# A fused attention and gated-MLP block: head sums in larger batches, a longer token ring, and another order of the first loads

## The chip, the cores and the metric

The kernel runs on one core of a Trainium2 chip. A core has five engines that run side by side, each through its own list of instructions in order: TensorE (PE, matrix products into PSUM), VectorE (DVE), ScalarE (ACT), GpSimd (POOL) and SyncE (SP), which here only issues DMA transfers. They meet through semaphores. SBUF is the working memory; PSUM has eight banks of 128 partitions by 512 fp32 values. The metric is the device time of one execution in microseconds, the median of some runs.

## The reference

x has 2048 tokens of 640 features. Everything is computed on the layer-normalised tokens, and two branches are added to x:

```python
x = A_x
xn = _layernorm(x, axis=-1)
return x + _A_ref(xn, A_wqkv, A_wo) + _B_ref(xn, B_w_gate, B_w_up, B_w_down)
```

Branch A is attention with 32 heads of 20 features, in which a token sees only eight keys: itself and the tokens 2, 4, ... 14 before it.

```python
off = jnp.arange(W) * dil                       # W = 8, dil = 2
idx = pos[:, None] - off[None, :]
logits = jnp.einsum("bhsd,bhswd->bhsw", q, kg) * scale      # kg: k gathered at idx
logits = jnp.where(mask[None, None, :, :], logits, -1e9)    # mask: idx >= 0
attn = _softmax(logits, axis=-1)
o = jnp.einsum("bhsw,bhswd->bhsd", attn, vg)                # vg: v gathered at idx
```

Branch B is (xn @ w_gate) * (xn @ w_up) @ w_down with 1536 inner features.

## The kernel before

**A planner orders everything.** The kernel's parts are generators that yield tasks (an engine, what is read and written, a priority, how many PSUM banks are needed). `Sched.run` simulates the engines with estimated durations, and at each step gives an engine the ready task of the best priority (a small number is better). What comes out is a fixed list of instructions for each engine, and the semaphore waits between them are derived from the tiles read and written (`deps_of`). The estimates set only the order; on the chip an engine waits for what is really missing, and everything behind it on that engine waits too.

**Tiling.** Tokens come in 16 tiles of 128 and 4 blocks (j) of 512. Features come in 5 chunks (c) of 128, so that a chunk of q, k or v holds 4 of each head's 20 features for all 32 heads.

**Stages, in the order in which the data needs them:**

1. *Front* (`front`, one for each tile t): the x tile is loaded into a ring `XST` of `NXS` = 8 slots. VectorE takes statistics (L511, L514), ScalarE a square root (L517), VectorE normalises into `XNS` (L521, L522). Tiles 0 to 4 are transposed by TensorE (L541) and copied out by VectorE (L549); tiles 5 to 15 are transposed by DMA (L556). The result is `XNT`, features on partitions. A tile from 8 on is loaded only when the tile eight before it has been normalised.
2. *Projections* (`mms`, L579): q and k of blocks 0 and 1 in small pieces as tiles come, then q and k of blocks 2 and 3, and v (`proj_v`) for each block; ScalarE empties the banks (L584). v goes to DRAM (`store_v`), since it is read back shifted.
3. *Head products and sums*: for each block and each half r of the eight key offsets, VectorE multiplies q with four shifted k (L702), one instruction for each chunk, into one of 8 product slots `PRD`. `logits` sums them over each head's features: 20 narrow matmuls (32 output columns, four abreast in the array) for one block and half, L718, into one bank, which ScalarE empties into `LOG` (L728). There are 8 such batches. A product slot is free again when its matmuls are done.
4. *Softmax* for two blocks at a time on VectorE, with the exponential on ScalarE; the weights move by DMA into `ATX`.
5. *Weighted values*: for each unit u = (block, chunk), 20 in all, four shifted pieces of v are loaded into a ring `VX`, VectorE multiplies them with the weights, which stand in two PSUM banks (L861), GpSimd adds pairs into `SV` (L866), and TensorE sums with 8 narrow matmuls a unit (`sums`, L905); ScalarE empties the bank into `OT` (L914). Two units make one batch.
6. *Gate and up* (`gu`, L945): for each block 12 groups of two times 5 matmuls; ScalarE empties the gate's bank, VectorE multiplies it with the up bank (L954).
7. *Output* (`dn`, L1000): for each block 8 groups of 17 matmuls (12 from branch B, 5 from `OT`); VectorE adds x (L1011) and SyncE stores. A block's outputs start when all 5 of its units are summed.

**Order of the start.** SyncE issues x tile 0, then the five chunks of the q weights one by one with x tile 2 between, then the k weights in two pieces with x tile 3 between; ScalarE's own queue issues x tile 1. TensorE meanwhile runs dummy matmuls on zeros (`warm`, L563): nine of 512 columns at the start and three behind the first tile's transposes.

Much memory is shared over time: `VST` (v before its store) and the ring `XST` lie in `OT`, the product slots in the down weights and others.

Of the kernel before, what the change touches and what calls it, by code (L numbers as in the profile page):

```python
# [3 lines left out]
FP32 = mybir.dt.float32  # L4
# [5 lines left out]
D = 640  # L10
# [9 lines left out]
NJ = 4  # L20
# [15 lines left out]
class _Op:  # L36
    __slots__ = ("eng", "fn", "deps", "needs_tick", "event", "pre_know", "dma", "name", "idx", "end", "group")

# [10 lines left out]
class Sched:  # L49
# [5 lines left out]
    def __init__(self, nc):  # L55
        self.nc = nc
        self.ops = []
        self.state = {}
        self.base = {}
        self.clock = {e: nc.alloc_semaphore(f"clk_{e}") for e in ("act", "pe", "dve", "pool")}  # L60
        self.n_dma = 0
        self.t = {"sp": 0.8, "act": 0.8, "pe": 1.26, "dve": 0.9, "pool": 0.8}
        self.t_lock = 0.0
        self.t_data = 0.0
        self.pe_mode = 0
        self.threads = []
        self.banks = {b: 0.0 for b in range(8)}
        self.seq = 0
        self.groups = {}

    def sbuf(self, name, shape, dtype, offset):
# [33 lines left out]
    def deps_of(self, eng, rk, wk):  # L105
        deps = {}
        inorder = eng in ("pe", "act", "dve")
        for k in rk:
            st = self.state.get(k)
            if st is not None and st[0] is not None:  # L110
                deps[st[0].idx] = st[0]
        for k in wk:
            st = self.state.get(k)
            if st is None:
                continue
            o, rds = st
            if o is not None and not (eng == "pe" and o.eng == "pe"):
                deps[o.idx] = o
            for q in rds:
                if inorder and q.eng == eng and not q.dma:  # L120
                    continue
                deps[q.idx] = q
        return deps

    def op(self, eng, fn, r=(), w=(), dma=False, name="", occ=None, lat=None, lock=False, nbytes=0, mode=0, group=None):
        X = _Op()
        X.eng, X.fn, X.name, X.dma, X.group = eng, fn, name, dma, group
        X.needs_tick, X.event, X.pre_know, X.idx = False, None, None, len(self.ops)
        rk = [k for a in r for k in self.keys(a)]
        wk = [k for a in w for k in self.keys(a)]  # L130
# [10 lines left out]
        if dma:  # L141
            self.t[eng] = start + (0.48 if occ is None else occ)
            self.t_data = max(self.t_data, start + 1.2) + nbytes / 280e3
            X.end = self.t_data + 0.8
        else:
            self.t[eng] = start + occ
            X.end = start + (occ if lat is None else lat)
# [190 lines left out]
def build_kernel(nc, A_x, A_wqkv, A_wo, B_x, B_w_gate, B_w_up, B_w_down, out):  # L338
# [5 lines left out]
    def sb(name, shape, dtype=BF16, at=None):  # L344
# [4 lines left out]
        if at is None:  # L349
# [13 lines left out]
    VST = sb("VST", [128, NJ, NCH, JB], at=a_ot)  # L363
    NXS = 8
    XST = sb("XST", [128, NXS, D], at=a_ot + 2 * NCH * JB * 2)
    a_qk = place[0]
    QT = sb("QT", [128, NJ, NCH, JB])
    KT = sb("KT", [128, NCH, VL])
    NVX = 5
    VX = sb("VX", [128, NVX, 4, VW], at=a_qk)  # L370
# [5 lines left out]
    PRD += [sb(f"PRD{5 + i}", [128, 4, JB]) for i in range(3)]  # L376
    NS = 3
    SV = [sb(f"SV{i}", [128, 4, JB], at=a_pr + i * 4096) for i in range(NS)]
    a_sc = place[0]
# [5 lines left out]
    RS = sb("RS", [128, 2, TS], at=a_sc + 4096)  # L385
    PV = [sb("PV0", [128, 2, 2, JB], FP32, at=a_qk + 20864), sb("PV1", [128, 2, 2, JB], FP32, at=a_qk + 20864 + 8192),
          sb("PV2", [128, 2, 2, JB], FP32, at=a_sc)]
    NP = len(PV)
    LOG = [sb(f"LOG{i}", [128, 2, W, TS]) for i in range(2)]
    HX = [sb(f"HX{i}", [128, JB], at=place[0] - 8192 + i * 1024) for i in range(8)]  # L390
    HX += [sb(f"HX{8 + i}", [128, JB]) for i in range(4)]
    ATX0 = sb("ATX0", [128, 2, 2, JB])
    ATX = [ATX0, sb("ATX1", [128, 2, 2, JB])]
    NXR = 3
    a_xr = place[0]
# [31 lines left out]
    def num(n, *k):  # L427
        return lambda: count.get(k, 0) >= n
# [23 lines left out]
    op("pool", lambda e: e.memset(KT[:, :, 0:PAD], 0.0), w=[KT[:, :, 0:PAD]], name="kpad", occ=0.3)  # L452

    def x_load(t, eng="sp"):
        dma(XST[:, t % NXS, :], xhbm[t * TS:(t + 1) * TS, :], w=[XST[:, t % NXS, :]], name=f"xld{t}", eng=eng)
        mark("x", t)
# [7 lines left out]
    def loads():  # L464
        def t(f, *a):
            return Task("sp", lambda: f(*a), prio=0)

        for t_ in range(4, NXS):
            yield t(x_load, t_)
        for t_ in range(NXS, NT):  # L470
            yield have("apply", t_ - NXS)
            yield t(x_load, t_)
            if t_ == NXS + 2:
                yield t(wqkv_load, 2)

# [12 lines left out]
    def late_loads():  # L488
        yield num(2 * NJ, "lg")

# [11 lines left out]
    def front(t):  # L502
        x, st = XST[:, t % NXS, :], STATS[:, t, 0:12]
        xs, mv = XNS[:, t % NXN, :], MV[:, t, 0:2]
# [49 lines left out]
        else:  # L554
            def dmat():
                op("sp", lambda e: e.dma_start_transpose(o, xs), r=[xs], w=[o], dma=True, name=f"dtr{t}", nbytes=200e3, occ=1.25)  # L556

# [3 lines left out]
    def warm(n):  # L561
        for _ in range(n):
            op("pe", lambda e: e.matmul(PS[:, 7, :], ZERO[:, 0:128], ZERO[:], start=True, stop=True),  # L563
               r=[ZERO[:]], w=[PS[:, 7, :]], name="warm", occ=0.4 if n > 3 else 0.25)

# [83 lines left out]
    def proj_v(j, m):  # L649
# [11 lines left out]
        for t in range(4 * j, 4 * j + 4):  # L661
            yield have("xnt", t)
        if j >= 2:
            for t in range(NT):
                yield have("apply", t)
        yield Task("pe", go, r=[WQKV[:, 2, 4, 0:64], XNT[:, NCH - 1, j * JB:(j + 1) * JB]], prio=30 + j, banks=1)
# [15 lines left out]
    def products():  # L682
        n = 0
        for j, r in pairs:
            slots = []
            for c in range(NCH):
                for which in (0, 1):
                    yield num(4, "qk", which, j, c)
                    if which == 1 and j > 0:
                        yield num(4, "qk", 1, j - 1, c)  # L690
                if n >= 8:
                    yield have("prd", n - 8)
                s = PRD[n % 8]
                base = KT[:, c, :]
# [10 lines left out]
                yield Task("dve", go, r=[q, rk], w=[s[:]], prio=20 + j, lock=True)  # L705
                slots.append((n, s))
                n += 1
            K.spawn(logits(j, r, slots))

    def logits(j, r, slots):  # L710
        hold = []

        def go(b):
            for c, (n, s) in enumerate(slots):
                for a in range(4):
# [5 lines left out]
                mark("prd", n)  # L721
            hold.append(b)

        dst = LOG[j // 2][:, j % 2, 4 * r:4 * r + 4, :]

        def ev():
            b = hold[0]
            X = op("act", lambda e: e.activation(dst, PS[:, b, :].rearrange("p (q s) -> p q s", q=4), ACT.Copy, scale=SCALE), r=[PS[:, b, :]], w=[dst],  # L728
                   name=f"lgev{j}_{r}", occ=0.58)
            K.free_bank(b, X)  # L730
# [6 lines left out]

        yield Task("pe", go, r=[slots[-1][1][:]], prio=9.5, banks=1, slack=0.5)
        bump("lg")
        yield Task("act", ev, r=[PS[:, hold[0], :]], w=[dst], prio=2)  # L740
        bump("logits", j // 2)

    def softmax(x):
# [35 lines left out]

        yield num(4, "logits", x)  # L780
        if x:
# [16 lines left out]
    def vx_loads():  # L798
        yield num(2 * NJ, "lg")
        for u in range(NU):  # L800
# [15 lines left out]

    at_bank = []
    used = [-3, -2, -1]

# [10 lines left out]
    def unit(u):  # L830
# [60 lines left out]
        mark("mul", u)  # L891
        if u % 2 == 1:
            K.spawn(sums((u - 1, u)))

    def sums(us):
# [22 lines left out]

        yield Task("pe", go, r=[SV[u % NS][:] for u in us], prio=9.7, banks=2, slack=0.7)
        yield Task("act", ev, r=[PS[:, b, :] for b in hold], prio=3)  # L920

    def gu(j):
# [5 lines left out]
        elif j == 1:  # L928
            for jj in range(NJ):
                yield num(NCH, "v", jj)  # L930
        elif j == 2:
            yield have("atx", 1)
        else:
            yield num(8, "dn", j - 3)
# [179 lines left out]
```

## Time and profile before

| | us |
|---|---|
| median of 3 runs (274.76 to 275.71) | 275.2 |
| the profiled execution, its own time | 276.79 |
| its span in the trace | 275.1 |

| engine | busy us | largest groups of instructions (line, busy us) |
|---|---|---|
| TensorE | 266.8 | gate and up L945 117.1; output L1000 84.5; projections L579 67.8; head sums L718 10.1; value sums L905 6.2; dummies L563 5.5 |
| VectorE | 222.9 | weighted values L861 92.8; products L702 46.1; gate times up L954 24.3 and more |
| GpSimd | 95.4 | pair sums L866 93.8 |
| ScalarE | 93.6 | emptying PSUM L584, L728, L914 |

Busy time of TensorE counts pipelined matmuls from start to modelled end, so a run of 20 is given some 0.1 to 0.2 us longer than the distance to the next start; distances between starts are the safer measure. How full the span is, in 40 slices of 6.9 us (a digit is the busy share in tenths):

```profile
PE   6997999999999999999999999999999999999995
...
DVE  4676789999999979999999999999799999423221
ACT  2355667555754245224243302221033201142000
POOL 1000000000000000197847976699656877500000
...
DMA  6959348802122899968423447535561012200101
```

Some transfers of the start, from issue to landing: x tile 0 (160 KB) 3.1 us from 0.81; x tile 1, on ScalarE's queue, 2.9 us from 0.81; the five q weight chunks (160 KB each) 2.9 to 5.1 us; k weights 5.9 (480 KB) and 6.2 us (320 KB); v weights (800 KB), issued at 12.42, 5.9 us.

### The profile page before, as it was taken

The numbers are of one execution on the slowest core, as the hardware profiler recorded it, in microseconds if no ns is written. First come the engines' busy times: TensorE is split into PE (matmuls) and PEld (weight loads), VectorE is DVE, ScalarE is ACT, GpSimd is POOL, SyncE is SP. The second block draws the span as 40 slices with busy tenths as digits, with TensorE's granted clock in tenths as the row PEclk, the third lists the DMA queues.
The fourth block names the chain that finished last, engine by engine and source line by source line (L and its number), as shares of the span: only waits on it lengthen the run. The fifth ranks groups of instructions, "written<-read, shape, count | busy, mean of one in ns | idle before, by whom it ended". The sixth has DMA issues, their size and how long they took to land.

```text
span 275.1 us, 4416 instructions
## 1 busy us (share of the span) xinstructions
PE 266.8 (97%) x1761; PEld 151.1 (55%) x1781; DVE 222.9 (81%) x285; ACT 93.6 (34%) x169; POOL 95.4 (35%) x57
## 2 busy tenths in 40 slices
PE   6997999999999999999999999999999999999995
PEld 2796965444444444444444576466744576444773
DVE  4676789999999979999999999999799999423221
ACT  2355667555754245224243302221033201142000
POOL 1000000000000000197847976699656877500000
PEclk9999999999999999999999999999999999999999
DMA  6959348802122899968423447535561012200101
GB/s 191 308 170 147 80 86 268 334 2 80 44 84 52 232 212 238 290 121 207 107 52 84 121 112 189 153 80 165 148 167 24 1 50 75 68 2 0 48 26 48
DMA packets 39492, 33.47 MB, mean 122 GB/s; under 512 B 15024, under 2 KB 38192, under 8 KB 39472
## 3 DMA queue, kind: packets, MB, share of 16 engines
q1 hardware_dynamic: 39328, 33.03, 45.6%
q8 instruction: 14, 0.23, 0.4%
q10 hardware_dynamic: 144, 0.16, 0.2%
q14 instruction: 6, 0.05, 0.1%
HBM read 25.07 MB, written 5.26 MB: 110 GB/s over the span
## 4 chain that ended last, share of the span: by engine, by line
PE 94%; DMA 3%; DVE 1%; issue 1%; ACT 0%; SPq 0%
PE PS L945 38%; PE PS L1000 27%; PE PS L579 22%; PE PS L718 3%; PE PS L905 2%; DMA XNT<-XNS 2%; DMA XST<-in_A_x_dram 1%; PE PS L541 1%; PE PS L563 0%; DVE XNT L549 0%; DVE XNS L522 0%; DVE STATS L511 0%; ACT SD L517 0%; DVE FOUT L1011 0%; DVE SD L521 0%
## 5 line engine op out<-in xcount | busy, mean ns | idle before, releaser
L866 POOL TENSOR_TENSOR SV<-PV 128x1024 bf16<-128x1024 f32 x40 | 93.8, 2358 | 87.8 <-DVE PV L861 87.6
L861 DVE TENSOR_TENSOR PV<-VX,PS 128x1024 f32<-128x1024 bf16 (+1 forms) x56 | 92.8, 1671 | 1.4 <-ACT PS L846 1.4
L579 PE MATMUL PS<-XNT,WQKV 128*128 128x512 bf16 (+2 forms) x473 | 67.5, 302 | 2.7 <-DMA XNT<-XNS 1.6
L945 PE MATMUL PS<-XNT,WG 128*128 128x512 bf16 x237 | 59.2, 379 | 0.2
L579 PEld LDWEIGHTS PS<-XNT,WQKV 128*128 128x128 bf16 x480 | 44.3, 115 | 25.6 <-DMA XNT<-XNS 2.1
L945 PE MATMUL PS<-XNT,WU 128*128 128x512 bf16 x230 | 57.9, 379 | 0.4
L702 DVE TENSOR_TENSOR PRD<-QT,KT 128x2048 bf16<-128x2048 bf16 x40 | 46.1, 1218 | 0.0
L1000 PE MATMUL PS<-WD,HT 128*128 128x320 bf16 x288 | 43.1, 299 | 0.0
L584 ACT ACTIVATE HT<-PS 128x512 bf16<-128x512 f32 x36 | 21.4, 596 | 54.8 <-PE PS L945 54.8
L945 PEld LDWEIGHTS PS<-XNT,WU 128*128 128x128 bf16 x240 | 23.1, 98 | 29.1 <-issue 1.7
L945 PEld LDWEIGHTS PS<-XNT,WG 128*128 128x128 bf16 x240 | 23.2, 98 | 28.7 <-issue 1.3
L954 DVE TENSOR_TENSOR HT<-HT,PS 128x512 bf16<-128x512 bf16 x36 | 24.3, 684 | 14.6 <-PE PS L945 14.4
L1000 PEld LDWEIGHTS PS<-WD,HT 128*128 128x128 bf16 x288 | 27.9, 98 | 12.3 <-issue 1.3
L1011 DVE TENSOR_TENSOR FOUT<-PS,XR 128x320 bf16<-128x320 f32 x32 | 15.6, 488 | 19.2 <-PE PS L1000 19.2
L1000 PE MATMUL PS<-WO,OT 128*128 128x320 bf16 x160 | 27.0, 299 | 0.0
L914 ACT ACTIVATE OT<-PS 128x512 bf16<-128x512 f32 x20 | 10.8, 596 | 35.6 <-PE PS L905 35.6
L736 POOL MEMSET LOG<- 32x6 bf16 (+6 forms) x7 | 0.4, 95 | 53.7 <-ACT LOG L728 53.7
L1000 PEld LDWEIGHTS PS<-WO,OT 128*128 128x128 bf16 x160 | 15.7, 98 | 6.1
L584 ACT ACTIVATE QT<-PS 128x512 bf16<-128x512 f32 (+1 forms) x22 | 12.3, 557 | 12.4 <-PE PS L579 12.4
L511 DVE BATCH_NORM_STATS2 STATS<-XST 128x6 f32<-128x320 bf16 x32 | 13.9, 477 | 2.7 <-DMA XST<-in_A_x_dram 2.7
L584 ACT ACTIVATE HX<-PS 128x512 bf16<-128x512 f32 x12 | 7.2, 597 | 25.7 <-PE PS L945 25.7
L584 ACT ACTIVATE KT<-PS 128x512 bf16<-128x512 f32 (+1 forms) x22 | 12.3, 557 | 7.9 <-PE PS L579 7.9
(43 smaller groups left out, 130.7 us busy)
## 6 DMA issues: line engine op xcount, KB each, us to landing
VX<-v_scratch SPq DMA_DIRECT2D x80, 130.0 KB, 2.9
v_scratch<-VST SPq DMA_DIRECT2D x4, 640.0 KB, 4.5
XR<-in_A_x_dram SPq DMA_DIRECT2D x16, 160.0 KB, 2.8
XST<-in_A_x_dram SPq DMA_DIRECT2D x15, 160.0 KB, 4.4
out_dram<-FOUT SPq DMA_DIRECT2D x15, 160.0 KB, 1.8
WG<-in_B_w_gate_dram SPq DMA_DIRECT2D x1, 1920.0 KB, 7.8
WU<-in_B_w_up_dram SPq DMA_DIRECT2D x1, 1920.0 KB, 11.8
WD<-in_B_w_down_dram SPq DMA_DIRECT2D x1, 1920.0 KB, 13.5
```

The lines of the kernel that those rows point to most:

```text
L511: op("dve", (lambda o, a: lambda e: e.bn_stats(o, a))(o, a), r=[a], w=[("st", t, i)], name=f"bn{t}_{i}", occ=0.49)
L579: op("pe", (lambda o, l, x, c, first: lambda e: e.matmul(o, l, x, start=first, stop=(c == NCH - 1)))(o, l, x, c, first), r=[l, x], w=[o], ...
L584: X = op("act", (lambda o, i: lambda e: e.activation(o, i, ACT.Copy))(o, i), r=[i], w=[o], name=name, occ=0.12 + n * 0.9e-3)
L702: op("dve", lambda e: e.tensor_tensor(s[:], qb, kv, ALU.mult), r=[q, rk], w=[s[:]], name=f"prod{j}_{r}_{c}", occ=1.15, lock=True)
L718: op("pe", (lambda o, x, a, c: lambda e: e.matmul(o, G[:], x, start=(c == 0), stop=(c == NCH - 1), tile_position=(0, 32 * a)))(o, x, a, c) ...
L861: op("dve", lambda e: e.tensor_tensor(p, vw, a, ALU.mult), r=[vv] + rk, w=[p], name=f"pv{u}_{x}_{r0}", occ=0.09 + 1.1 * nr)
L866: X = op("pool", lambda e: e.tensor_tensor(o, p[:, :, 0, :], p[:, :, 1, :], ALU.add), r=[p[:]], w=[o], name=f"pva{u}_{x}", occ=2.36, lock= ...
L914: X = op("act", (lambda o, b: lambda e: e.activation(o, PS[:, b, :], ACT.Copy))(o, b), r=[PS[:, b, :]], w=[o], name=f"oev{u}", occ=0.58)
L945: op("pe", (lambda l, x, c: lambda e: e.matmul(PS[:, b, :], l, x, start=(c == 0), stop=(c == NCH - 1)))(l, x, c), r=[l, x], w=[PS[:, b, :] ...
L954: X = op("dve", lambda e: e.tensor_tensor(h, h, PS[:, hold[1], :], ALU.mult), r=[h, PS[:, hold[1], :]], w=[h], name=f"h{m}_{j}", occ=0.65)
L1000: op("pe", (lambda l, x, i: lambda e: e.matmul(PS[:, b, 0:DHALF], l, x, start=(i == 0), stop=(i == n - 1)))(l, x, i), r=[l, x], w=[PS[:, b ...
L1011: X = op("dve", lambda e: e.tensor_tensor(o, PS[:, b, 0:DHALF], xr, ALU.add), r=[PS[:, b, :], xr], w=[o], name=f"fin{t}_{nb}", occ=0.49)
```

## The change

Seven edits go together:

- **Head sums once a block**: `logits` takes both halves of a block, ten slots, into two banks: 4 batches of 40 narrow matmuls. There are twelve product slots, the four new ones in memory that is free at that time; every twelfth product waits for the last token tile to be transposed, and gate/up of block 1 for all head sums (a slot lies in its `HT`).
- **Value sums for three units**: six batches of three units (three banks) and a last one of two. `SV` has five slots instead of three, `VX` four instead of five.
- **Token ring of twelve**: x tiles 4 to 11 are issued without waiting, then the v weights, then tiles 12 to 15. The ring now lies also where v of block 1 is put, so v of block 1 waits for tiles 8 to 11.
- **First loads**: all on SyncE's queue; q weights in two pieces (3 and 2 chunks), k weights in one.
- **Dummies**: 22 of 256 columns at the start, three of 256 later.
- **Planner**: a transposing DMA is taken to land 1.3 us later than before.
- **Dependences**: a VectorE instruction that overwrites what a VectorE instruction four or more places earlier read now waits for it by semaphore.

```diff
-                if inorder and q.eng == eng and not q.dma:
+                if inorder and q.eng == eng and not q.dma and (eng != "dve" or self.n_eng[eng] - q.nth < 4):
...
-            X.end = self.t_data + 0.8
+            X.end = self.t_data + 0.8 + extra
...
-    NXS = 8
-    XST = sb("XST", [128, NXS, D], at=a_ot + 2 * NCH * JB * 2)
+    NXS = 12
+    XST = sb("XST", [128, NXS, D], at=a_ot + NCH * JB * 2)
...
-    NVX = 5
+    place[0] += 64
+    NVX = 4
...
-    NS = 3
+    NS = 5
...
+    PRD += [sb("PRD8", [128, 4, JB], at=a_ra + 3 * NCH * D * 2)]
...
+    PRD += [sb("PRD9", [128, 4, JB], at=place[0])]
...
+    PRD += [sb("PRD10", [128, 4, JB], at=place[0] - 4096), sb("PRD11", [128, 4, JB], at=place[0])]
+    NPR = len(PRD)
...
         for t_ in range(4, NXS):
             yield t(x_load, t_)
+        yield t(wqkv_load, 2)
         for t_ in range(NXS, NT):
             yield have("apply", t_ - NXS)
             yield t(x_load, t_)
-            if t_ == NXS + 2:
-                yield t(wqkv_load, 2)
...
-                op("sp", lambda e: e.dma_start_transpose(o, xs), r=[xs], w=[o], dma=True, name=f"dtr{t}", nbytes=200e3, occ=1.25)
+                op("sp", lambda e: e.dma_start_transpose(o, xs), r=[xs], w=[o], dma=True, name=f"dtr{t}", nbytes=200e3, occ=1.25, extra=1.3)
...
-            op("pe", lambda e: e.matmul(PS[:, 7, :], ZERO[:, 0:128], ZERO[:], start=True, stop=True),
+            op("pe", lambda e: e.matmul(PS[:, 7, 0:QB], ZERO[:, 0:128], ZERO[:, 0:QB], start=True, stop=True),
...
-        if j >= 2:
-            for t in range(NT):
-                yield have("apply", t)
+        for t in range(NT) if j >= 2 else range(8, 12) if j else ():
+            yield have("apply", t)
...
-                if n >= 8:
-                    yield have("prd", n - 8)
-                s = PRD[n % 8]
+                if n % NPR == NPR - 1:
+                    yield have("xnt", NT - 1)
+                if n >= NPR:
+                    yield have("prd", n - NPR)
+                s = PRD[n % NPR]
...
-            K.spawn(logits(j, r, slots))
+            if r == 0:
+                K.spawn(logits(j, slots))
...
-        yield Task("pe", go, r=[slots[-1][1][:]], prio=9.5, banks=1, slack=0.5)
+        yield Task("pe", go, r=[slots[-1][1][:]], prio=9.5, banks=2, slack=0.5)
...
-        if u % 2 == 1:
-            K.spawn(sums((u - 1, u)))
+        pend.append(u)
+        if len(pend) == 3 or u == NU - 1:
+            K.spawn(sums(tuple(pend)))
+            pend.clear()
...
-        yield Task("pe", go, r=[SV[u % NS][:] for u in us], prio=9.7, banks=2, slack=0.7)
+        yield Task("pe", go, r=[SV[u % NS][:] for u in us], prio=9.7, banks=len(us), slack=0.7)
...
+            yield num(NJ, "lg")
...
     x_load(0)
-    x_load(1, eng="act")
+    x_load(1)
+    wqkv_load(0, 0, 3)
+    wqkv_load(0, 3, NCH)
+    x_load(2)
+    wqkv_load(1)
+    x_load(3)
     K.t["act"] = 2.1
-    for c in range(NCH):
-        wqkv_load(0, c, c + 1)
-        if c == 2:
-            x_load(2)
-    wqkv_load(1, 0, 3)
-    x_load(3)
-    wqkv_load(1, 3, NCH)
-    warm(9)
+    warm(22)
```

More of the change, by code (lines that the diff above doesn't have):

```diff
@@ L36 @@
 class _Op:
-    __slots__ = ("eng", "fn", "deps", "needs_tick", "event", "pre_know", "dma", "name", "idx", "end", "group")
+    __slots__ = ("eng", "fn", "deps", "needs_tick", "event", "pre_know", "dma", "name", "idx", "end", "group", "nth")
 class Task:
@@ L69, in __init__ @@
         self.groups = {}
+        self.n_eng = {e: 0 for e in ENGINES}
     def sbuf(self, name, shape, dtype, offset):
@@ L123, in deps_of, with op @@
         return deps
-    def op(self, eng, fn, r=(), w=(), dma=False, name="", occ=None, lat=None, lock=False, nbytes=0, mode=0, group=None):
+    def op(self, eng, fn, r=(), w=(), dma=False, name="", occ=None, lat=None, lock=False, nbytes=0, mode=0, group=None, extra=0.0):
         X = _Op()
@@ L128, in op @@
         X.needs_tick, X.event, X.pre_know, X.idx = False, None, None, len(self.ops)
+        X.nth = self.n_eng[eng]
+        self.n_eng[eng] += 1
         rk = [k for a in r for k in self.keys(a)]
@@ L376, in build_kernel @@
     PRD += [sb(f"PRD{5 + i}", [128, 4, JB]) for i in range(3)]
-    NS = 3
-    SV = [sb(f"SV{i}", [128, 4, JB], at=a_pr + i * 4096) for i in range(NS)]
+    NS = 5
+    SV = [sb(f"SV{i}", [128, 4, JB], at=a_pr + i * 4096) for i in range(3)]
+    SV += [sb("SV3", [128, 4, JB], at=a_qk + 33024), sb("SV4", [128, 4, JB], at=a_qk + 33024 + 4096)]
     a_sc = place[0]
@@ L385, in build_kernel @@
     RS = sb("RS", [128, 2, TS], at=a_sc + 4096)
-    PV = [sb("PV0", [128, 2, 2, JB], FP32, at=a_qk + 20864), sb("PV1", [128, 2, 2, JB], FP32, at=a_qk + 20864 + 8192),
+    PV = [sb("PV0", [128, 2, 2, JB], FP32, at=a_qk + 16640), sb("PV1", [128, 2, 2, JB], FP32, at=a_qk + 16640 + 8192),
           sb("PV2", [128, 2, 2, JB], FP32, at=a_sc)]
     NP = len(PV)
+    PRD += [sb("PRD8", [128, 4, JB], at=a_ra + 3 * NCH * D * 2)]
     LOG = [sb(f"LOG{i}", [128, 2, W, TS]) for i in range(2)]
     HX = [sb(f"HX{i}", [128, JB], at=place[0] - 8192 + i * 1024) for i in range(8)]
+    PRD += [sb("PRD9", [128, 4, JB], at=place[0])]
     HX += [sb(f"HX{8 + i}", [128, JB]) for i in range(4)]
@@ L452, in build_kernel, with xslot @@
     op("pool", lambda e: e.memset(KT[:, :, 0:PAD], 0.0), w=[KT[:, :, 0:PAD]], name="kpad", occ=0.3)
+    def xslot(t):
+        return t + 4 if t < 8 else t - 8
     def x_load(t, eng="sp"):
-        dma(XST[:, t % NXS, :], xhbm[t * TS:(t + 1) * TS, :], w=[XST[:, t % NXS, :]], name=f"xld{t}", eng=eng)
+        dma(XST[:, xslot(t), :], xhbm[t * TS:(t + 1) * TS, :], w=[XST[:, xslot(t), :]], name=f"xld{t}", eng=eng)
         mark("x", t)
@@ L488, in late_loads @@
     def late_loads():
-        yield num(2 * NJ, "lg")
+        yield num(NJ, "lg")
         def go():
@@ L502, in front @@
     def front(t):
-        x, st = XST[:, t % NXS, :], STATS[:, t, 0:12]
+        x, st = XST[:, xslot(t), :], STATS[:, t, 0:12]
         xs, mv = XNS[:, t % NXN, :], MV[:, t, 0:2]
@@ L562, in warm @@
         for _ in range(n):
-            op("pe", lambda e: e.matmul(PS[:, 7, :], ZERO[:, 0:128], ZERO[:], start=True, stop=True),
-               r=[ZERO[:]], w=[PS[:, 7, :]], name="warm", occ=0.4 if n > 3 else 0.25)
+            op("pe", lambda e: e.matmul(PS[:, 7, 0:QB], ZERO[:, 0:128], ZERO[:, 0:QB], start=True, stop=True),
+               r=[ZERO[:]], w=[PS[:, 7, :]], name="warm", occ=0.2 if n > 3 else 0.12)
     def wcols(which, c, m):
@@ L684, in products @@
         for j, r in pairs:
-            slots = []
+            if r == 1:
+                slots = []
             for c in range(NCH):
@@ L705, in products, with logits, go @@
                 yield Task("dve", go, r=[q, rk], w=[s[:]], prio=20 + j, lock=True)
-                slots.append((n, s))
+                slots.append((n, s, r, c))
                 n += 1
-            K.spawn(logits(j, r, slots))
-    def logits(j, r, slots):
+            if r == 0:
+                K.spawn(logits(j, slots))
+    def logits(j, slots):
         hold = []
-        def go(b):
-            for c, (n, s) in enumerate(slots):
+        def go(*bs):
+            for n, s, r, c in slots:
+                b = bs[1 - r]
                 for a in range(4):
@@ L721, in go, with dst, ev @@
                 mark("prd", n)
[L722 to L729, printed above, removed]
+            hold.extend(bs)
+        def dst(r):
+            return LOG[j // 2][:, j % 2, 4 * r:4 * r + 4, :]
+        def ev(r):
+            b, d = hold[1 - r], dst(r)
+            X = op("act", lambda e: e.activation(d, PS[:, b, :].rearrange("p (q s) -> p q s", q=4), ACT.Copy, scale=SCALE),
+                   r=[PS[:, b, :]], w=[d], name=f"lgev{j}_{r}", occ=0.58)
             K.free_bank(b, X)
@@ L736, in ev @@
                         op("pool", (lambda m: lambda e: e.memset(m, NEG))(m), w=[m], name=f"mask{w}", occ=0.2)
-        yield Task("pe", go, r=[slots[-1][1][:]], prio=9.5, banks=1, slack=0.5)
+        yield Task("pe", go, r=[slots[-1][1][:]], prio=9.5, banks=2, slack=0.5)
         bump("lg")
-        yield Task("act", ev, r=[PS[:, hold[0], :]], w=[dst], prio=2)
+        for r in (1, 0):
+            yield Task("act", lambda: ev(r), r=[PS[:, hold[1 - r], :]], w=[dst(r)], prio=2)
         bump("logits", j // 2)
@@ L778, in move @@
             mark("atx", x)
-        yield num(4, "logits", x)
+        yield num(2, "logits", x)
         if x:
@@ L798, in vx_loads @@
     def vx_loads():
-        yield num(2 * NJ, "lg")
+        yield num(NJ, "lg")
         for u in range(NU):
@@ L817, in build_kernel @@
     at_bank = []
+    pend = []
     used = [-3, -2, -1]
@@ L930, in gu @@
                 yield num(NCH, "v", jj)
+            yield num(NJ, "lg")
         elif j == 2:
```

## The prediction

> **What bounds the kernel now.** I read the engine shares first, then the chain that ended last, then TensorE's waits, then TensorE's timeline around its small batches.
>
> ```profile
> PE 266.8 (97%) x1761; PEld 151.1 (55%) x1781; DVE 222.9 (81%) x285; ACT 93.6 (34%) x169; POOL 95.4 (35%) x57
> ...
> PE 94%; DMA 3%; DVE 1%; issue 1%; ACT 0%; SPq 0%
> ```
>
> TensorE is busy 97% and carries 94% of the chain. From 24.64 us on the chain is TensorE alone, up to the last output add at 272.34. So only three things can shorten the span: TensorE's start, its waits, and time in which it is busy but slow.
>
> ```profile
> PE PS L579 <- DMA XNT<-XNS: 1.6, 1, 1.6
> PE PS L563 <- DVE EPSC L440: 1.3, 1, 1.3
> PE PS L541 <- DVE XNS L522: 0.8, 1, 0.8
> PE PS L579 <- DVE XNT L549: 0.6, 1, 0.6
> ```
>
> These are all of its waits: four, all before 25 us (a fifth entry is 0.2 of issue). The first is the only large one inside the work: the projections stop for the first transposing DMA, which was issued at 20.17 and landed at 24.59, 4.42 us where the median is 2.6.
>
> ```profile
> 7.88 2.21 PE L579 MATMUL PS<-XNT,WQKV 128*128 128x128 bf16 x20
> ...
> 10.96 1.31 PE L579 MATMUL PS<-XNT,WQKV 128*128 128x128 bf16 x20 [0.59 <-DVE XNT L549]
> ...
> 97.62 1.24 PE L945 MATMUL PS<-XNT,WG 128*128 128x512 bf16 x5
> 98.80 1.26 PE L718 MATMUL PS<-PRD,G 128*32 128x512 bf16 x20
> 99.99 1.25 PE L945 MATMUL PS<-XNT,WU 128*128 128x512 bf16 x5
> 101.08 0.38 PE L945 MATMUL PS<-XNT,WG 128*128 128x512 bf16 x1
> ```
>
> The first two rows are the same 20 matmuls: 2.21 us early, 1.31 later, so TensorE runs at about half speed until roughly 10 us. The next four are start times around one batch of head sums. Five matmuls of 512 columns take 1.09 (99.99 to 101.08), 0.216 each; a narrow matmul, four abreast, then costs 0.054. The group before the batch takes 1.18 to the batch's start, 0.10 too much; the batch 1.19 where 20 x 0.054 = 1.08, 0.11 too much. **One excursion into narrow matmuls costs 0.21 us.** The value batch at 127.07 gives the same: 0.09 before it, and 0.55 for 8 x 0.054 = 0.43.
>
> **The change part by part.**
>
> *Fewer batches.* Head sums go from 8 batches of 20 to 4 of 40, value sums from 10 of 8 to six of 12 and one of 8. The matmuls stay; 18 excursions become 11. 7 x 0.21 = **1.5 us gone**, all on the path. Ends 1.3 (a long batch might pay a little at its second bank) and 1.5.
>
> A rule speaks against this part. The Trainium skill, TensorEngine Tiling (Array Packing), section PSUM Bottleneck, says that tiling speeds up TensorE but not the emptying of PSUM, which may then become the limit. A value batch will hold three banks and a head batch two, and ScalarE empties a bank in 0.596 us (L914). Two of eight banks hold the attention weights, so three remain for the gate and up groups while a batch is emptied. By the rule, TensorE would stop for the extra bank: six value batches and four head batches, 10 x 0.596 = 6.0 us lost. By the row: after today's two-bank batch the next groups start at 127.62 and 128.71, with no gap at all; emptying three banks takes 1.79 us, in which TensorE starts two groups of 1.08, and three banks are there for them. I take 0 and keep 6.0 as the other end.
>
> *Later sums.* The value sums of block 1 now come with unit 11 instead of unit 9: two units, about 11 us (178.37 to 189.34), so the output products of block 1 start that much later. What covers it is work that needs no later sum. The chain has some 300 of the 480 gate/up matmuls done by 154.3, so 180 x 0.216 = 38.9 us remain then, and 19.2 for each output block (154.89 to 174.12, less one batch). Until 189.3 TensorE needs 35.0 us of work and has 38.9 + 19.2; until the last sums at 240.2 it needs 85.9 and has 38.9 + 3 x 19.2 = 96.5. **Cover 10.6 us**, less the 4.3 that TensorE gains: 6. Cost 0; without cover, each us that the VectorE/GpSimd chain is late counts fully. That chain runs ahead: it gains some 3 us itself (below), and loses about 1.1 because the last head batch is twice as long (softmax waits for both banks; the vector products of unit 0 that follow are delayed as long).
>
> *Twelve product slots.* A block's ten slots come free only with its batch, so VectorE has two spare ones, 2 x 1.14 us (18 products in 20.53), where a batch starts within one group (1.08) and frees its first slot 0.2 later, with some 0.5 of planner's slack: 1.8 against 2.3. Cost 0; if it stalls, 3 x 1 us of VectorE time under the cover above. The twelfth slot waits for the last transposed tile; before, the twelfth product ran at about 54, and that tile was issued at 40.7. No wait. The added VectorE self-waits are on instructions at least four back: long done, 0.
>
> *Start.* The first x tile's landing (3.88) is shared with the second, which the ScalarE queue issued at the same time and which landed first, at 3.7. On one queue the first comes alone, I estimate 0.4 earlier. But TensorE cannot use it: 22 dummies of half size take 22 x 0.213 (half of 0.427 measured: nine in 3.84) = 4.69, from 1.26 to 5.95, and the transposes start behind them, 6.0 instead of 6.09. The gain follows: the three dummies behind the transposes end at about 7.2 instead of 8.09, the first tile's copy at 7.2, and the first projection starts at 7.24 instead of 7.88. Its 20 matmuls take 1.3 instead of 2.2 if the clock is open by then. Then tile 1 binds: its normalised rows are ready at 8.3 (8.47 now), transposed by 8.85, VectorE copies behind the statistics of tile 2, by 9.6; second projection 9.65 instead of 10.96. **1.3 us gone**; after it TensorE was never idle until 23.06, so the gain is kept. The three fifths and two fifths of the first weights (480 and 320 KB, with 320 KB of x ahead): the trace's bytes per half microsecond add up to that total at 6.3, landing 6.9 at latest, in time; the second weights (800 KB) land at 10.2 by the same sum, wanted at 11; x tile 3 is behind them, at 10.7, wanted at 10.7. SyncE issues 20 loads instead of 24 ahead of the transposes; none waits for a late tile.
>
> Whether the clock opens: the Trainium skill, TensorE: Matmul & The Clock Gate, Part 1, says that one wholly busy window of 3.41 us, free-running, opens it. The row: 3.84 us of dummies did not, then 0.81 idle, and full speed came 3.8 after the restart. By the row's 3.8 alone, the unbroken run from 1.26 opens it at 5.1 to 6; by the rule anywhere from 4.67 to 8.09, for which eight of the 20 stay slow, 0.3 less. I take open at 7.2. Ends: 0.65 (not open before 9.8) and 2.0 (VectorE's order lets the copy go first).
>
> *First transposing DMA.* The planner now allows 1.3 us more for it. At 23.06 TensorE had only one of block 0's five value groups behind it (first VST evacuation at 23.10), so 4 x 1.08 = 4.3 us of work was ready but queued behind the wait. With the later estimate these go first: they cover the 1.6. Their weights, landed at 18.4 now, come before 18. Block 1's values now wait for tiles 8 to 11 normalised (32.4 now), but come after 36. What is late next is tile 7, with 5 us of projections ahead. **1.5 us gone**; ends 0 and 1.6. It also frees ScalarE, which stood 2.26 behind that wait and held VectorE's tile 8 for 1.72: VectorE's chain is some 3 us earlier.
>
> **Sum.** 1.5 + 1.3 + 1.5 = 4.3. The profiled execution took 276.79 for a span of 275.1; 275.1 - 4.3 = 270.8 span, 272.5 executed. The median of the plain runs is 275.2, so **270.9**. A check from below: TensorE's matmuls at full pace add to 257, eleven excursions 2.3, start 7.2, tail 2.8: 269.3, and 1.5 of small gaps and the wait for tile 1.
>
> **Rivals.**
> 1. *Only the batches count*: the clock opens at 9.8 as now and the planner leaves the wait where it is: 275.2 - 1.5 - 0.65 = 273.0. For it: the wait is set by an order that I can't see, and the window's phase is luck. Against: the transfer estimate is raised by just the missing size. The part of "it does not do what it says" is here.
> 2. *More*: the first copy goes ahead of tile 2's statistics, saving 2.0 there, and gaps of 0.05 around the batches go too: 275.2 - 1.5 - 2.0 - 1.6 - 0.9 = 269.2. Against: near the floor above.
> 3. *Slower*: the extra bank per batch, 0.596 x 10 = 6.0 lost, gives 270.9 + 6.0 = 276.9. It decides from 0.43 per batch on. For: the rule; ScalarE's order puts the sums' banks ahead of the gate's. Against: no gap behind a batch now, ScalarE 34% busy.
>
> **Chances.** Forecast 0.64 (270.0 to 272.0), rival 1 0.18, rival 2 0.12, rival 3 0.06. The range 269.0 to 273.2 takes in the first two rivals' values. Within 0.3% (0.8 us, what can't be told from no change) lies only a half-effective rival 3: faster 0.92, same 0.03, slower 0.05.
>
> **What would show it.** Right: the wait on the transposing DMA gone from TensorE's list; second projection near 9.7; 11 narrow batches, each 0.21 over its matmuls; no waits of a gate group on ScalarE. Wrong: gate matmuls idle behind an evacuation of OT or LOG; TensorE waiting for the last value sums before output block 3; first projections still 0.107 each.

## The result, and the profile after

| | before | after |
|---|---|---|
| median of the plain runs on record | 275.45 (274.76 to 276.0, 4 runs) | 272.89 (272.79 to 273.05, 4 runs) |
| the profiled execution, its own time | 276.79 | 272.93 |
| its span | 275.1 | 271.0 |

The ratio is 0.9909, with a 95% interval of 0.9884 to 0.9934. The change gains 2.6 us of the median; the forecast was 4.3 and 270.9. The result also lies outside the forecast's own band, 270.0 to 272.0. The two profiled executions differ by 3.9 us in time and 4.1 in span. So the sum fits the two traces and not the medians, and the question is why.

TensorE's waits in the trace of after (waiter, whom it waited for, us in total, times, longest):

```profile
PE PS L574 <- DVE EPSC L449: 1.3, 1, 1.3
PE PS L590 <- DVE XNT L560: 0.7, 1, 0.7
```

The wait on the transposing DMA (1.6 before) is gone, and so is the one for the first tile's rows. TensorE's timeline at the start (start, duration, engine, line, operation, tiles, count, idle before):

```profile
5.93 0.74 PE L552 MATMUL PS<-IDENT,XNS 128*128 128x128 bf16 x5
6.47 0.75 PE L574 MATMUL PS<-ZERO 128*128 128x256 bf16 x3
7.26 1.31 PE L590 MATMUL PS<-XNT,WQKV 128*128 128x128 bf16 x20
8.41 0.44 PE L552 MATMUL PS<-IDENT,XNS 128*128 128x128 bf16 x5
9.57 1.31 PE L590 MATMUL PS<-XNT,WQKV 128*128 128x128 bf16 x20 [0.72 <-DVE XNT L560]
```

The first projection starts at 7.26 (foreseen 7.24) and runs at full speed; the second starts at 9.57 (foreseen 9.65, before 10.96). And around one head batch and one value batch, in TensorE's timelines of two stretches:

```profile
94.86 1.24 PE L966 MATMUL PS<-XNT,WG 128*128 128x512 bf16 x5
96.04 2.34 PE L733 MATMUL PS<-PRD,G 128*32 128x512 bf16 x40
98.31 1.25 PE L966 MATMUL PS<-XNT,WU 128*128 128x512 bf16 x5
```

```profile
131.10 0.83 PE L925 MATMUL PS<-SV,SEL 128*32 128x512 bf16 x12
131.86 1.25 PE L966 MATMUL PS<-XNT,WU 128*128 128x512 bf16 x5
132.95 1.24 PE L966 MATMUL PS<-XNT,WG 128*128 128x512 bf16 x5
```

40 narrow matmuls take 2.27 from start to next start, 0.11 over 40 x 0.054; the 12 take 0.76, 0.11 over 0.65. (A unit has four narrow matmuls, not the eight of stage 5 above: the trace of before has 80 at L905 for 20 units.) The entry is 0.10 as before (94.86 to 96.04 for 1.08). A longer batch costs the same 0.21 as a short one, and the groups after a batch of three banks follow 1.09 apart: no wait for a bank. So far the trace follows the prediction. It also has a stop that was not foreseen: a gate group near 112 starts 0.3 us late, and the experiments come back to it.

### The profile page after: what moved, and what is told of

It reads as the page before. It is cut to its first block, busy times and chain, and to the rows that moved or that the text cites. A ratio compares the mean times of both kernels' runs of the same rounds, so it can differ in the third digit from the quotient of the medians.

```text
span 271.0 us, 4452 instructions
## 1 busy us (share of the span) xinstructions
PE 265.9 (98%) x1794; PEld 153.4 (57%) x1794; DVE 224.5 (83%) x285; ACT 93.4 (34%) x169; POOL 96.4 (36%) x57
## 3 DMA queue, kind: packets, MB, share of 16 engines
HBM read 25.07 MB, written 5.26 MB: 112 GB/s over the span
## 4 chain that ended last, share of the span: by engine, by line
PE 91%; DVE 6%; issue 1%; ACT 0%; DVEq 0%
PE PS L966 33%; PE PS L1021 27%; PE PS L590 24%; PE PS L733 3%; PE PS L925 2%; PE PS L574 2%; DVE SM L762 2%; DVE PV L879 1%; DVE HT L975 1%; DVE RS L782 1%; PE PS L552 1%; DVE M L762 0%; DVE XNT L560 0%; DVE STATS L522 0%; DVE LOG L773 0%
## 5 line engine op out<-in xcount | busy, mean ns | idle before, releaser
L884 POOL TENSOR_TENSOR SV<-PV 128x1024 bf16<-128x1024 f32 x40 | 94.8, 2379 | 87.0 <-DVE PV L879 86.8
L590 PE MATMUL PS<-XNT,WQKV 128*128 128x512 bf16 (+2 forms) x480 | 66.6, 299 | 0.8 <-DVE XNT L560 0.7
L966 PE MATMUL PS<-XNT,WU 128*128 128x512 bf16 x240 | 59.7, 379 | 0.0
L590 PEld LDWEIGHTS PS<-XNT,WQKV 128*128 128x128 bf16 x480 | 43.5, 113 | 23.4 <-DVE XNT L560 1.6
L975 DVE TENSOR_TENSOR HT<-HT,PS 128x512 bf16<-128x512 bf16 x36 | 23.9, 683 | 12.7 <-PE PS L966 12.7
L595 ACT ACTIVATE VST<-PS 128x512 bf16<-128x512 f32 x20 | 11.7, 597 | 8.1 <-PE PS L590 8.1
```

The lines of the kernel that those rows point to most:

```text
L590: op("pe", (lambda o, l, x, c, first: lambda e: e.matmul(o, l, x, start=first, stop=(c == NCH - 1)))(o, l, x, c, first), r=[l, x], w=[o], ...
L595: X = op("act", (lambda o, i: lambda e: e.activation(o, i, ACT.Copy))(o, i), r=[i], w=[o], name=name, occ=0.12 + n * 0.9e-3)
L884: X = op("pool", lambda e: e.tensor_tensor(o, p[:, :, 0, :], p[:, :, 1, :], ALU.add), r=[p[:]], w=[o], name=f"pva{u}_{x}", occ=2.36, lock= ...
L966: op("pe", (lambda l, x, c: lambda e: e.matmul(PS[:, b, :], l, x, start=(c == 0), stop=(c == NCH - 1)))(l, x, c), r=[l, x], w=[PS[:, b, :] ...
L975: X = op("dve", lambda e: e.tensor_tensor(h, h, PS[:, hold[1], :], ALU.mult), r=[h, PS[:, hold[1], :]], w=[h], name=f"h{m}_{j}", occ=0.65)
```

## The experiments

All ratios are to the kernel before, run beside each kernel on the same chip. The three values of before's span belong to three chips, so kernels of different sets are compared by their ratios, not by their times. Twelve runs were made, two of them of before and after unchanged. "Span" is the median span of the executions.

| kernel | what it is | ratio (95% interval) | span | before's span beside it |
|---|---|---|---|---|
| b_again | before, unchanged | 1.0004 (0.9992 to 1.0017) | 273.35 | 273.4 |
| batch_only | both larger batches alone | 0.9973 (0.9961 to 0.9986) | 272.4 | 273.4 |
| start_only | first loads and dummies alone | 1.0006 (0.9995 to 1.0017) | 273.65 | 273.4 |
| dtr_only | transpose estimate alone | 0.9942 (0.9925 to 0.9958) | 271.9 | 273.4 |
| a_again | after, unchanged | 0.9902 (0.9877 to 0.9927) | 270.9 | 273.65 |
| a_old_start | after with before's start | 0.9911 (0.9883 to 0.9939) | 271.3 | 273.65 |
| a_no_extra | after without the estimate | 0.9965 (0.9953 to 0.9977) | 272.7 | 273.65 |
| a_warm19 | after with 19 dummies | 0.989 (0.9866 to 0.9913) | 270.55 | 273.65 |
| head_only | head batches alone | 0.9998 (0.9989 to 1.0007) | 273.15 | 273.5 |
| value_only | value batches alone | 0.9985 (0.9975 to 0.9994) | 272.7 | 273.5 |
| ne_sm | a_no_extra, products behind softmax | 0.9907 (0.989 to 0.9924) | 270.75 | 273.5 |
| w19_sm | a_warm19, products behind softmax | 0.9891 (0.9874 to 0.9908) | 270.35 | 273.5 |

**Is the profiled execution of before a usual one?** The same kernel again, 22 executions, with 48 more of before beside it.

> The kernel before, unchanged. Theory (T): the profiled execution of before, 275.1 us of span, was a long one; its start and its first transposing DMA cost more there than in most runs. Then the span here is some 1 to 1.5 us shorter, 273.5 to 274.2, the ratio is 1.00, and the difference lies before 25 us. Rival (U): the span is near 275 again and the plain runs are shorter than the profiled one for a reason outside of the span.

Measured: 119 spans of before (these 22 and the 97 beside the three sets) lie from 273.0 to 275.3; 100 of them at or below 274.0, 19 above, with the median at 273.5. The profiled one, 275.1, is among the longest. So T holds for the plain runs. The new profile fell at 274.6, again among the long ones, so it shows what a long one looks like and not a usual one: its first 20 projections take 2.18 us, because TensorE runs at half speed until 9.8 us ("its clock opens late"), and it waits 1.1 for the transposing DMA. An early opening with nine dummies, where these 20 take about 1.3, appears in the traces of value_only, dtr_only, batch_only and head_only, whose dummies are those of before. That the usual executions of before are of this kind is inferred: both traces of before itself are late. TensorE's timeline in value_only:

```profile
6.24 0.81 PE L568 MATMUL PS<-ZERO 128*128 128x512 bf16 x3
7.04 1.33 PE L584 MATMUL PS<-XNT,WQKV 128*128 128x128 bf16 x20
8.21 0.44 PE L546 MATMUL PS<-IDENT,XNS 128*128 128x128 bf16 x5
9.36 1.31 PE L584 MATMUL PS<-XNT,WQKV 128*128 128x128 bf16 x20 [0.70 <-DVE XNT L554]
```

The clock is open here before the dummies behind the transposes, with nine old dummies of 512 columns, and the second projection starts at 9.36, earlier than in after. Of the seven traces with the old dummies, three open late (20 matmuls in 2.2 to 2.3 us: before, b_again, a_old_start) and four early (about 1.3). Of the seven with 19 or 22 fine dummies (of 256 columns), six are open by the first projection, and w19_sm opens some 0.4 us into it (20 matmuls in 1.48).

**One part alone, each.** The larger batches:

> Before with the head and value sums in larger batches (and the slots and dependences that they need), nothing else. T: 7 excursions of 0.21 us less, 1.5 us, ratio 0.9946, the same in each run. Rival (P): the third bank costs TensorE up to 0.6 us per batch, ratio 1.00 or above.

```diff
-            K.spawn(logits(j, r, slots))
+            if r == 0:
+                K.spawn(logits(j, slots))
...
-        if u % 2 == 1:
-            K.spawn(sums((u - 1, u)))
+        pend.append(u)
+        if len(pend) == 3 or u == NU - 1:
+            K.spawn(sums(tuple(pend)))
+            pend.clear()
```

Measured: 0.6 us in the median, 1.0 in the span. Faster, so not P; but short of T's 1.5. Where the rest went is followed below.

The start alone, all of its loads and dummies:

> Before with the first loads and the dummies of the change, nothing else. T: second projection near 9.6 instead of 10.96 us where the clock opened late before; against the plain runs of before only 0.3 to 1.0 us, as they already open earlier in part, ratio 0.996 to 0.999. U: the full 1.3 us, ratio 0.995.

```diff
-    x_load(1, eng="act")
+    x_load(1)
+    wqkv_load(0, 0, 3)
+    wqkv_load(0, 3, NCH)
...
-    warm(9)
+    warm(22)
```

Measured: no gain. Its trace has the second projection at 9.20, even before T's 9.6, and yet its spans (272.6 to 274.1) are no shorter than usual ones of before. U is out, and T was too hopeful. TensorE's waits in that trace, and the two groups of projections:

```profile
PE PS L579 <- DMA XNT<-XNS: 1.4, 1, 1.4
PE PS L563 <- DVE EPSC L440: 1.3, 1, 1.3
PE PS L579 <- DVE XNT L549: 1.0, 2, 0.7
...
9.20 1.31 PE L579 MATMUL PS<-XNT,WQKV 128*128 128x128 bf16 x20 [0.72 <-DVE XNT L549]
...
22.96 2.27 PE L579 MATMUL PS<-XNT,WQKV 128*128 128x256 bf16 x19 [1.42 <-DMA XNT<-XNS]
```

The wait for the first transposing DMA is still there and ends at 22.96 us. It does not hide what the start wins, for its end moves with the start: the second projection and the end of this wait stand at 9.36 and 22.98 in value_only, at 9.80 and 23.33 in batch_only, at 9.99 and 23.30 in head_only, and in the two late traces of before at 10.94 and 24.11 (b_again) and at 10.96 and 24.64. A late opening thus costs 0.8 to 1.7 us at this place. Against value_only, whose old start opened early, the new start is 0.16 ahead at the second projection and 0.02 at the end of the wait. There is next to nothing to win where the clock opens early anyway.

The planner's estimate alone:

> Before with only the planner's estimate for a transposing DMA raised by 1.3 us. T: TensorE runs more value groups before the first tile that comes by DMA and does not wait for it; 1.5 us against the profiled execution of before, but less against its plain runs if the 4.42 us landing was an outlier: 0 to 1 us, ratio 0.997 to 1.0. U: 1.5 us, ratio 0.9945.

```diff
-name=f"dtr{t}", nbytes=200e3, occ=1.25)
+name=f"dtr{t}", nbytes=200e3, occ=1.25, extra=1.3)
```

Measured: 1.6 us in the median, 1.5 in the span. U is right here and T wrong: the wait is no accident of one execution. All six traces that have before's order at this place, early or late, wait 1.1 to 1.6 there; this one shows no such wait.

**The change with one part undone.** To see whether the start counts once that wait is gone, and how the change itself spreads:

> The changed kernel, unchanged, many executions beside before. Theory (T2: before's span has two levels, near 273.3 in about four of five executions and 274.4 to 275.1 in the others, where TensorE's clock opens late; the profiled execution of before was one of the others; the unbroken dummies take the second level away). Then all executions lie within 0.5 us and the ratio is 0.991. Rival (U2: the change has the same two levels): a fifth of them is 1 to 1.5 us longer.

> The changed kernel with the first loads and dummies of before. T2: the lower level is the same as the changed kernel's or up to 0.3 us lower, since with the clock open early nine dummies end sooner than 22, but about one execution in five is some 1.2 us longer; ratio to before about 0.991. Rival (S: the start is worth its 1.3 us once the wait on the transposing DMA is gone): 1.3 us longer than the changed kernel, ratio 0.996.

```diff
-    warm(22)
+    warm(9)
```

(and the first loads as before). Measured: after's six spans are 270.7, 270.7, 270.8, 271.0, 271.0 and 271.7; with the old start 270.7, 270.9, 271.0, 271.6, 271.7 and 272.4. The lower ends agree, so S is out: the full 1.3 us is not there. The medians differ by 0.4 us, with ratios whose intervals overlap. The upper end is longer by 0.7; the profiled one of a_old_start is the 272.4, with its 20 matmuls in 2.26 us and the second projection at 11.13. T2 holds in kind, but six executions don't fix the share of late ones. After isn't free of a spread either: one of its six is 0.8 above their median, more than T2's 0.5, so U2 is not excluded by them.

> The changed kernel without the raised estimate for transposing DMAs. T2: TensorE waits again 1.0 to 1.7 us for the first tile that comes by DMA, 1.4 us longer than the changed kernel, ratio to before 0.996. Rival (R: the ring of twelve and the early v weights already bring the transposes in time): no wait, ratio 0.991.

Measured: 1.8 us longer than after, as T2 said, but not for T2's reason. TensorE's waits in that trace:

```profile
PE PS L966 <- DVE HT L975: 1.5, 1, 1.5
...
PE PS L590 <- DMA XNT<-XNS: 0.2, 1, 0.2
```

The wait on the transposing DMA is 0.2: R is right that it is nearly gone with the old estimate, but not for R's reason and not in the time. The tile comes no sooner (the wait ends at 22.94, in start_only at 22.96); TensorE has some 1.2 us more work in front of it. Instead the gate and up groups stand for 1.5 us, until 115.26, waiting for VectorE. What held VectorE, in its timeline of that trace:

```profile
101.43 0.69 DVE L762 TENSOR_TENSOR M<-LOG 128x1024 bf16<-128x1024 bf16 x1
102.15 2.78 DVE L762 TENSOR_TENSOR M<-M 128x512 bf16<-128x512 bf16 x2
...
109.69 3.18 DVE L762 TENSOR_TENSOR SM<-SM 128x512 f32<-128x512 f32 x2
```

These pairs take 0.75 and 1.15 in before. GpSimd's pair sums ran at 101.60 and 108.60. Some 0.4 us more is lost in the first value batch of that trace (131.55), which stops until a pair sum of GpSimd is done. After has the overlap once, and no such stop, in the timeline of all engines:

```profile
104.51 1.22 DVE L762 TENSOR_TENSOR SM<-LOG 128x1024 f32<-128x1024 bf16 x1
...
104.68 3.26 POOL L884 TENSOR_TENSOR SV<-PV 128x1024 bf16<-128x1024 f32 x1 [50.30 <-DVE PV L879]
...
105.76 3.18 DVE L762 TENSOR_TENSOR SM<-SM 128x512 f32<-128x512 f32 x2
...
111.27 1.24 PE L966 MATMUL PS<-XNT,WU 128*128 128x512 bf16 x5
...
111.91 1.88 DVE L975 TENSOR_TENSOR HT<-HT,PS 128x512 bf16<-128x512 bf16 x3
...
112.65 1.04 PE L966 MATMUL PS<-XNT,WG 128*128 128x512 bf16 x4
```

GpSimd's sum takes 0.9 longer than its usual 2.36, and the next VectorE instruction, which starts at 105.76, takes 2.73 where it took 0.69 in before: it ends half a microsecond after the sum is over (107.94). The gate product behind the softmax (L975) then starts only at 111.91, and TensorE's group at 112.65 comes 1.38 after the one before instead of 1.08: the 0.3 us seen in after. The Trainium skill, SBUF — State Buffer, section SBUF: two separate sides, says that VectorE with two SBUF inputs and GpSimd share one pair of ports as an exclusive lock: whoever starts first blocks the other for a whole instruction. The times fit that: GpSimd is late by the rest of the first VectorE instruction, VectorE then by GpSimd's whole sum. No run here looks at the ports themselves. The planner has a model of that lock, but nothing enforces it on the chip.

**Head or value batches?** The two halves of batch_only, each alone:

> Before with the larger head batches alone (twelve slots, the added dependences). Theory (E: an excursion costs 0.21 us, but the head batches also bring the first pair sum of GpSimd beside VectorE's softmax, which costs TensorE 0.3 us, and some 0.6 us at the end of the program): 4 x 0.21 = 0.84 less on TensorE, ratio about 0.999 to 1.0, wait of a gate group for VectorE of 0.3 us near 113. Rival (F: the 0.3 and 0.6 come from the value batches): 0.84 less, ratio 0.997, no such wait.

> Before with value batches of three units alone (five sum slots, the added dependences). E: 3 x 0.21 = 0.63 less, ratio 0.9977, no wait near 113. F: 0.63 less minus the losses, ratio about 1.0, with the wait or the longer end.

Measured: head_only has the wait of 0.3 us near 113.7 and the pair sum of 3.26 us (106.26) beside softmax; value_only has neither, and its first pair sum is at 114.56. E is right there. But the longer end belongs to the value batches: GpSimd's last two semaphore instructions stand 0.08 us apart in before and head_only, and 0.41 in value_only and every other kernel with batches of three. Of this 0.33 only 0.1 reaches the span: from the end of the last output add to the end of the span it is 2.29 us in before and in head_only, and 2.42 in value_only. Time outside the span is 1.70 in before, 1.86 in head_only, 1.92 in value_only. Head_only's trace has one more loss, in its first value batch:

```profile
125.12 1.05 PE L919 MATMUL PS<-SV,SEL 128*32 128x512 bf16 x8
125.78 0.10 PEld L919 LDWEIGHTS PS<-SV,SEL 128*32 128x32 bf16 x2 [0.54 <-POOL SV L880]
126.11 1.25 PE L960 MATMUL PS<-XNT,WG 128*128 128x512 bf16 x5
```

The batch takes 0.99 to the next start instead of 0.55, since its last weight loads (PEld) wait for a pair sum. By these terms head_only should gain 0.84 - 0.3 - 0.4 = 0.1 of span, where 0.35 was measured and nothing clear in time, and value_only 0.63 - 0.1 = 0.5, where 0.8 was measured (0.5 in time). What is left, 0.2 to 0.3 each, is not explained, nor is why the end is longer.

**The overlap taken away.** The first weighted products are put behind the second softmax, so that no pair sum can start beside it:

```diff
         yield have("atx", 0)
+        yield have("sm", 1)
```

> The changed kernel without the raised transpose estimate, and with the first weighted products put behind the second softmax in VectorE's order, so that no pair sum of GpSimd runs beside it. In a_no_extra two pair sums fell beside softmax instructions that took 2.0 us longer each, and TensorE waited 1.5 us for a gate product behind them. Theory (C: that overlap is what the missing estimate costs): the wait is gone, 1.4 to 1.7 us less than a_no_extra, ratio to before 0.991. Rival (Q: the gate products are late for another reason): still 1 us or more of wait, ratio 0.9965.

Measured: 1.7 us less than a_no_extra, each against before on its own chip (1.9 as the times stand), span 270.75, the softmax pairs at 0.75 and 1.15 again, and no wait of a gate group: Q is out and C fits. One thing the run does not part from the overlap: the edit also takes four weighted products, 4.7 us of VectorE's time, out of its order ahead of the late gate products. The two lengthened pairs of a_no_extra alone held VectorE 4.1 us, more than the 1.5 that TensorE waited. Without the raised estimate this kernel is as fast as after (0.9907 against 0.9902 and 0.9909).

**A better version.** In after, tile 0 was ready at 5.26 and stood behind dummies until 5.93.

> The changed kernel with 19 dummies at the start instead of 22. In its trace tile 0 was normalised at 5.26 us and the transposes waited behind dummies until 5.93. 19 end at 5.31: T2: everything after comes up to 0.6 us earlier, 0.3 to 0.6 us less span, ratio 0.989. Rival (G: the three dummies are needed to keep the clock's window full): same or a second level 1 us above.

```diff
-    warm(22)
+    warm(19)
```

Measured: 0.3 us less than after in the median, with ratios whose intervals overlap; spans 270.5 to 271.0, no second level in six executions. The transposes start at 5.34, but TensorE then waits 0.9 for the q weights and the second projection comes at 9.50, so most of the 0.6 is lost; the two profiled spans are equal, 271.0.

> The changed kernel with 19 dummies and with the first weighted products behind the second softmax. C: 0.3 us less than with 19 dummies alone, ratio 0.988, the 0.3 us wait near 112 gone; the value sums end later but stay hidden. Rival (H: the chain of weighted products then runs out of cover): TensorE waits for the last value sums, ratio 0.99 or above.

Measured: 272.15 us, the shortest time of all, but on another chip than 19 dummies alone (272.45) and after (272.78, a_again). Against before on its own chip it gains 3.0, where those gained 2.9 and 2.6, so C's 0.3 over 19 dummies alone is not shown. The wait near 112 is gone, as VectorE's timeline shows (1.15 again for the pair), and H didn't come. In this trace the q weights came in time too (second projection at 8.97), so its short profiled span, 270.1, is not due to the softmax alone.

```profile
103.17 1.23 DVE L762 TENSOR_TENSOR SM<-LOG 128x1024 f32<-128x1024 bf16 x1 [0.78 <-ACT LOG L777]
104.42 1.15 DVE L762 TENSOR_TENSOR SM<-SM 128x512 f32<-128x512 f32 x2
```

## Why the prediction was right or wrong

The direction and the range were right, and so were the mechanisms of the batches and of the transposing DMA; the size was 4.3 for 2.6. The result, 272.89, lies beside rival 1's 273.0, but by luck: rival 1 kept the wait on the transposing DMA and gave the start 0.65, while the runs show the wait gone and the start worth next to nothing.

- **The start, 1.3: measured as nothing alone** (start_only, 1.0006 of before, from 0.9995 to 1.0017), and as 0 to 0.4 within the change. This is the mis-sized term. The working, 10.96 to 9.65, is right for the profiled execution (9.57). But that execution was a long one, in which the clock opened late; its loss was taken off a median of runs that, by their spans, mostly don't have it. The numbers gave a warning: the profiled time, 276.79, lay above all three plain runs shown (274.76 to 275.71), and the 20 slow matmuls were read as the rule. The prediction's figure for the profiled execution, 272.5, is near the measured 272.93. The Trainium skill, TensorE: Matmul & The Clock Gate, Part 1, says that the window runs free and that the number of slow matmuls at the start differs between runs of one kernel. The traces agree: with the same nine dummies full speed came at 4.1 us in dtr_only and at 9.8 in before. The prediction used the page to place the opening in after and not to doubt the one in before.
- **The transposing DMA, 1.5: right**, by dtr_only, 1.5 in the span and 1.6 in the median. Within the whole change, though, the same edit acts in another way: without it (a_no_extra) the wait on the DMA is only 0.2, and TensorE waits 1.5 for a gate product instead. That the terms add up below is in part luck.
- **The batches, 1.5: the term is right on TensorE and too large in the sum.** Eleven excursions of 0.21 remain. Together with their slots the larger batches gain 1.0 of span. Of the 1.5, 0.3 goes to the softmax that a pair sum blocks and 0.1 to the later end of the span. The prediction had costed the reordering of VectorE's work at nothing because it lay under cover; it reached TensorE by the gate products queued behind the softmax. Of time outside the span, 0.1 to 0.4 more is lost (batch_only 2.1, after 1.9, before 1.7).
- **Costed at nothing, and rightly**: the third bank (no wait on an evacuation after a batch: rival 3 didn't come), the later output block, the twelve slots; TensorE's waits in after name none of them. The ring of twelve was not run alone.

Usual spans add up: 273.5 less 1.5 for the estimate, 1.0 for the batches and nothing for the start gives 271.0, which is after's.

## What to carry to other kernels

Compare the profiled execution with the plain runs before a stall of it is priced: a loss that comes by chance in fewer than half of the executions need not show in the median at all. Before a later wait is said to swallow an earlier gain, see whether its end moves with the start: here it did, from 22.96 to 24.64. And where an instruction of one engine lengthens another engine's, a planner's model of it is not enough; the order of instructions or a semaphore must keep them apart.

## What the runs showed of the hardware

- Nine dummies of 3.84 us, with an idle gap of 0.4 to 1.3 us behind them, were followed by a first projection at full speed in four traces of seven; 19 or 22 fine ones in six of seven, and in the seventh, w19_sm, full speed came 0.4 us into it.
- A pair sum on GpSimd beside softmax instructions on VectorE lengthened one of these by 2.0 us (0.69 to 2.73), and itself by up to 0.9.
- A batch of 8, 12, 20 or 40 narrow matmuls costs TensorE the same 0.20 to 0.21 us over its matmuls, where nothing it reads is late.
- Time outside the span isn't fixed: 1.67 to 1.76 on average for the kernels with the old value and head batches, 1.79 to 2.11 for those with either of the new.
